# Second product of the second MLP by Strassen's algorithm in an attention, MLP, MLP kernel on one core

## Chip, core and metric

The kernel runs on one core of one Trainium2 chip. The metric is the device time of one launch in microseconds (us), the median of several runs. The engines are PE (TensorE, matrix products; its weight loads are PEld), DVE (VectorE), ACT (ScalarE), POOL (GpSimd), and SP, whose queue issues all the DMAs.

## What is computed

```python
def _attn_ref(q, k, v, tau) -> np.ndarray:
    scale = 1.0 / np.sqrt(q.shape[-1])
    scores = scale * np.matmul(q, k.transpose(0, 1, 3, 2))
    thresh = np.max(scores, axis=-1, keepdims=True) - tau
    scores = np.where(scores >= thresh, scores, -1000000000.0)
    scores = scores - np.max(scores, axis=-1, keepdims=True)
    attn = np.exp(scores)
    attn = attn / (np.sum(attn, axis=-1, keepdims=True) + 1e-09)
    return np.matmul(attn, v).astype(np.float32)
...
def _moe_ref(x, w_in, w_out, alpha) -> np.ndarray:
    h = x @ w_in
    g = np.maximum(h, 0.0) + alpha * np.minimum(h, 0.0)
    return (g @ w_out).astype(np.float32)
...
def _moe2_ref(x, w_in, w_out) -> np.ndarray:
    h = x @ w_in
    g = h - np.tanh(h)
    return (g @ w_out).astype(np.float32)
...
    x = np.ascontiguousarray(attn_out.transpose(0, 2, 1, 3)).reshape(B * S, H * D)
    x = _moe_ref(x=x, **moe_kwargs)
    return _moe2_ref(x=x, **moe2_kwargs)
```

All of it is float32: 4 batches of 8 heads with 576 rows of 64, so 2304 tokens of 512; either MLP goes from 512 to 2048 and back.

## The kernel before

The 2304 tokens are nine blocks of 256 (`BLK`, `NBLK`). A fast matrix product takes operands rounded to the type `fp32r`, so each float32 operand is split into a rounded part hi and the rest lo, and a product is three: hi·hi, hi·lo, lo·hi. The 64 visits of the attention (a batch, a query block of 256 and a head each; `attend`) and 16 visits for the last 64 queries of two heads (`attend_left`) run softmax over rows of 576: row maximum, threshold, exponential, mask with row sum, guard, reciprocal, normalisation (`softmax`), then transposes on PE and the product with v (`products`). For the first `WHOLE` visits that product is one exact float32 product without any split (`one`), for the first `RAW` the scores are (`raw`); later visits use split operands. As soon as all eight heads of a block are there, the first MLP's work on that block runs between the attention's instructions.

An MLP block is eight pairs of inner chunks (`NPAIR`; a pair is 2 x 128 of the 2048 inner columns). `h_pair` makes a pair's first product, 24 products of 256 columns into the PSUM bank `hp`; then come the activation function into `mr` (ACT and DVE), the rounded copy `gh` (line 278) and the rest `gl` (line 283). `acc_pair` makes the second product from `gh`, `gl` and the weights. In the first MLP that is 24 products of 256 columns (line 957), in the second 12 products of 512 columns into `acc[0]` and `acc[1]` (line 949). `LEAD = 2`: the second product of a pair stands two pairs behind its first. After the eighth pair ACT copies `acc` out (`drain`) and SP stores it.

The weights come as 64-bit words of float64 numbers, which lines 333 to 351 turn into float32 (`rebias`, `three`, `ends_`, `middle`); then `hi` and `lo` split them (`piece`). Those of the second MLP take the places of the first's as these come free, so they are prepared in the stretch after the attention.

The order on every engine is written out ahead of time by a planner (`Plan.order`). Each operation has engines that may do it with an assumed cost (`any_of`, `either`: ACT, DVE or POOL), a rank (a number that grows with the place in the program, shifted by the constants `OFF`, `MLP_PE`, `MLP_G`, `PREP`, `PA`, `PB`, `XR`), and what it reads, writes and takes of buffers (`BUFS`). The planner always issues the operation that can start first, of several the one with the lowest rank; `POOL_PEN`, `ACT_PEN` and `DVE_PEN` are added when it compares engines. It takes POOL and a DVE operation that reads SBUF alone as excluding each other (`port_free`). 280 products on zeros (`warm`) fill PE where nothing else can run; they are used up within the first 150 us.

Of the kernel before, what the change touches and what calls it, by code (L numbers as in the profile page):

```python
# [22 lines left out]
P = 128  # L23
# [34 lines left out]
DVE_PEN = 0.9665  # L58
OFF = {"S": 22.48, "M": -53.36, "TH": -421.88, "E": -13.37, "X": -179.21, "R": -223.53, "N": 37.71, "T": 278.13, "H": -180.15, "L": -303.91, "AV": 69.42, "XC": -10.5, "XH": 126.9}
# [3 lines left out]
    "rkv": 1, "rq": 2, "ks": 3, "qs": 2, "vs": 3, "e": 2, "st": 2, "eT5": 1, "xt": 1, "rw": 4, "raw0": 2, "raw1": 4, "tw": 2,  # L63
    "x0": 2, "x1": 2, "mr": 1, "pair": 1, "xl": 1, "gh": GB, "gl": GB, "o": 2,
# [8 lines left out]
class Plan:  # L73
# [9 lines left out]
    def add(self, engines, rank, emit, reads=(), writes=(), banks=(), takes=(), lag=0.0, after=(), port=False):  # L83
# [19 lines left out]
        for tag, _ in takes:  # L103
            if tag != "rw":
                if tag in self.takers:
                    order.add(self.takers[tag])
                self.takers[tag] = n
        deps.discard(n)
        self.ops.append((engines, rank, emit, deps, order - deps, banks, takes, lag, "DVE" in engines and not banks and engines["DVE"] > 0.1))
        return n  # L110

    def order(self):
# [41 lines left out]
        issued = []  # L154
        pen = {"ACT": ACT_PEN, "DVE": DVE_PEN, "POOL": POOL_PEN}
        while len(issued) < n:
            best = None
            for e, cand in ready.items():
# [35 lines left out]
                key = (t + (pen[e] if len(ops[i][0]) > 1 else 0), fin)  # L194
# [34 lines left out]
def attention_mlp_mlp(ctx: ExitStack, tc: tile.TileContext, kv, q0, q1, tau, w1i, w1o, alpha, w2i, w2o, out):  # L229
# [37 lines left out]


# [43 lines left out]
    def piece(l, kind, qd, c, rank):  # L312
# [3 lines left out]
        raw, t, dst = ("raw", n), ("tw", n), ("w", (l, kind, qd))  # L316
# [37 lines left out]

        def hi(e):
# [48 lines left out]
    def prep(v, rank):  # L404
# [720 lines left out]
```

## Time and profile before

| | us |
|---|---|
| median of 3 runs (lowest, highest) | 1168.94 (1168.88, 1170.43) |
| the profiled execution, its own time | 1169.88 |
| its span | 1168.1 |
| PE busy in the span | 1141.2 (98%) |
| DVE, ACT, POOL busy | 662.9, 663.6, 525.5 |

A busy PE instruction lasts until its last column has left the array, so records of neighbours overlap: what an instruction costs PE is the distance from its start to the next start. On the other engines neighbours overlap by less than 0.1 us. The stages are the attention with most of the first MLP in it (0 to about 660 us), the rest of the first MLP (to about 760) and the second MLP.

### The profile page before, as it was taken

Reading aid. Unit: us, or ns where it says so; the run is one execution under the profiler, and the core shown is the slowest. Engines: PE = TensorE matmul, PEld = TensorE weight load, DVE = VectorE, ACT = ScalarE, POOL = GpSimd, SP = SyncE. Lnnn points to the kernel's source line nnn. Section 1 sums busy time; section 2 is a strip of 40 time slices with the busy share of each in tenths; the row PEclk is TensorE's granted clock in tenths of the full one; section 3 lists DMA queues with packets and bytes.
Section 4 is the critical chain, followed back from the end, with each engine's and each line's share of the span. In section 5 each row is a group of like instructions: output and inputs, shape, how many; then the busy total and the mean of one; then the engine's idle time right before and its main releaser. Section 6 shows DMA issues by size and latency. Waiting matters only on the chain.

```text
span 1168.1 us, 21647 instructions
## 1 busy us (share of the span) xinstructions
PE 1141.2 (98%) x8388; PEld 1051.9 (90%) x8388; DVE 662.9 (57%) x1388; ACT 663.6 (57%) x1277; POOL 525.5 (45%) x498
## 2 busy tenths in 40 slices
PE   8999999999999999999999999999999999999998
PEld 6777789899999999999999999999899999999997
DVE  5887787888887877878877665782111111111110
ACT  5887887677776767767677565664222233222221
POOL 2565564544555525556535375875233233233221
PEclk9999999999999999999999999999999999999999
DMA  6645533212122302132121353451011011010000
GB/s 177 188 159 160 159 107 100 55 49 64 54 65 84 86 13 80 54 92 81 46 70 41 95 163 127 141 167 55 1 37 36 1 36 37 1 37 18 1 19 19
DMA packets 55847, 86.88 MB, mean 74 GB/s; under 512 B 18624, under 2 KB 33984, under 8 KB 55744
## 3 DMA queue, kind: packets, MB, share of 16 engines
q1 hardware_dynamic: 55744, 85.49, 24.2%
q8 instruction: 66, 1.08, 0.4%
q14 instruction: 37, 0.30, 0.1%
HBM read 75.51 MB, written 9.96 MB: 73 GB/s over the span
## 4 chain that ended last, share of the span: by engine, by line
PE 72%; DVE 15%; ACT 8%; issue 3%; DMA 2%; SPq 1%; POOL 0%; DVEq 0%; ACTq 0%; POOLq 0%
PE hp L896 29%; PE acc L949 17%; PE acc L957 11%; PE sc L720 3%; DVE e L565 3%; PE pt L615 3%; DVE eT L283 3%; PE sc L689 2%; DVE st L553 2%; DMA rw<-in_w1i_dram 2%; ACT eT L278 1%; ACT e L561 1%; DVE st L570 1%; PE sc L681 1%; DVE mr L917 1%
## 5 line engine op out<-in xcount | busy, mean ns | idle before, releaser
L896 PE MATMUL hp<-x,ihi 128*128 128x256 f32 x2304 | 426.4, 284 | 1.7 <-DVE mr L917 1.6
L896 PEld LDWEIGHTS hp<-x,ihi 128*128 128x128 f32 x2304 | 358.9, 189 | 9.3 <-issue 1.4
L283 POOL TENSOR_TENSOR gl<-mr,gh 128x512 fp32r<-128x512 f32 x144 | 193.7, 1345 | 360.0 <-ACT gh L278 340.3
L896 PE MATMUL hp<-x,ilo 128*128 128x256 f32 x1152 | 323.9, 281 | 0.0
L915 DVE TENSOR_TENSOR mr<-hp,mr 128x512 f32<-128x512 f32 x72 | 49.8, 691 | 325.0 <-ACT mr L908 325.0
L896 PEld LDWEIGHTS hp<-x,ilo 128*128 128x128 f32 x1152 | 217.5, 189 | 0.0
L908 ACT ACTIVATE mr<-hp 128x512 f32<-128x512 f32 x72 | 43.1, 598 | 223.4 <-PE hp L896 223.4
L957 PE MATMUL acc<-gh,ohi 128*128 128x256 f32 x576 | 168.2, 292 | 0.5 <-ACT o L278 0.5
L957 PE MATMUL acc<-gl,ohi 128*128 128x256 f32 x576 | 161.8, 281 | 0.0
L957 PE MATMUL acc<-gh,olo 128*128 128x256 f32 x576 | 161.6, 281 | 0.0
L565 DVE SCALAR_TENSOR_TENSOR e<-sc,st,e 128x576 f32<-128x576 f32 x144 | 115.2, 814 | 21.1 <-ACT e L561 9.6
L278 ACT ACTIVATE gh<-mr 128x512 fp32r<-128x512 f32 x133 | 83.8, 630 | 73.9 <-DVE mr L915 48.8
L553 DVE TENSOR_REDUCE st<-sc 128x1 f32<-128x576 f32 x144 | 106.0, 749 | 17.4 <-PE sc L681 6.5
L949 PE MATMUL acc<-ohi,gl 128*128 128x512 f32 x288 | 113.8, 395 | 0.0
L949 PE MATMUL acc<-olo,gh 128*128 128x512 f32 x288 | 113.7, 395 | 0.0
L949 PE MATMUL acc<-ohi,gh 128*128 128x512 f32 x288 | 113.5, 394 | 0.0
L561 ACT ACTIVATE e<-sc,st 128x576 f32<-128x576 f32 x144 | 103.8, 739 | 10.8 <-DVE st L553 8.3
L957 PEld LDWEIGHTS acc<-gh,ohi 128*128 128x128 f32 x576 | 109.0, 189 | 0.9 <-ACT o L278 0.8
L957 PEld LDWEIGHTS acc<-gl,ohi 128*128 128x128 f32 x576 | 108.7, 189 | 0.0
L957 PEld LDWEIGHTS acc<-gh,olo 128*128 128x128 f32 x576 | 108.5, 188 | 0.0
L615 PE MATMUL pt<-ident,e 128*128 128x128 f32 x576 | 88.6, 276 | 6.4 <-ACT e L278 2.2
L278 ACT ACTIVATE e<-e,st 128x576 f32<-128x576 f32 x95 | 71.9, 771 | 40.3 <-DVE st L573 40.0
(91 smaller groups left out, 1948.5 us busy)
## 6 DMA issues: line engine op xcount, KB each, us to landing
rkv<-in_kv_dram SPq DMA_DIRECT2D x36, 288.0 KB, 2.8
rw<-in_w1i_dram SPq DMA_DIRECT2D x16, 512.0 KB, 4.8
rw<-in_w1o_dram SPq DMA_DIRECT2D x16, 512.0 KB, 4.0
rw<-in_w2i_dram SPq DMA_DIRECT2D x16, 512.0 KB, 4.5
rw<-in_w2o_dram SPq DMA_DIRECT2D x16, 512.0 KB, 3.5
rkv<-in_kv_dram SPq DMA_DIRECT2D x44, 160.0 KB, 2.9
ks<-in_kv_dram SPq DMA_DIRECT2D x20, 288.0 KB, 3.0
x1d<-o SPq DMA_DIRECT2D x18, 256.0 KB, 2.1
```

The lines of the kernel that those rows point to most:

```text
L278: e.activation(out=out_, in_=in_, func=AF.Copy, **({} if scale is None else {"scale": scale}))
L283: e.tensor_tensor(out=out_, in0=in_, in1=hi.bitcast(F32), op=ALU.subtract)
L553: e.tensor_reduce(out=T[st][:, 0, j:j + 1], in_=x(s), axis=AX.X, op=ALU.max, negate=True)
L561: e.activation(out=weights(j), in_=x(s), func=AF.Exp, bias=T[st][:, 0, j:j + 1], scale=1.0)
L565: e.scalar_tensor_tensor(out=w_, in0=x(s), scalar=T[st][:, 1, j:j + 1], in1=w_, op0=ALU.is_ge, op1=ALU.mult, accum_out=T[st][:, 2, j:j + 1])
L615: e.transpose(pt[:, c, :], x[:, c * P:(c + 1) * P], ident)
L720: e.matmul(po, lhsT=vf[:, c], rhs=T[g][part][:, c, :], start=(c + part == 0), stop=False)
L896: e.matmul(hp[:, k, :], lhsT=weight(l, "i", part, f // 4)[:, c, (f % 4) * P:(f % 4 + 1) * P], rhs=T[f"x{x}", m][:, c, :], start=(n0 + n == ...
L908: e.activation(out=T[r], in_=hp, func=AF.Tanh)
L915: e.tensor_tensor(out=T[r], in0=hp, in1=T[r], op=ALU.subtract)
L949: e.matmul(acc[t], lhsT=g[:, k, t * P:(t + 1) * P], rhs=w, start=(f == 0 and n == 0), stop=(f == NF - 1 and n == 2),)
L957: e.matmul(acc[t][:, (c % 2) * BLK:(c % 2 + 1) * BLK], lhsT=w[:, c * P:(c + 1) * P], rhs=g[:, k, :], start=(f == 0 and n == 0 and c % 2 == ...
```

## The change

In the second MLP a pair is a 2 x 2 problem: two halves of 128 tokens, two chunks of the inner dimension, two halves of 256 output columns. For six of the eight pairs (`STRASSEN`) its second product is made in seven products instead of eight, in Winograd's form of Strassen's algorithm: four sums of quarters of `mr` (`combine`, tile `gs`, 128 x 128 each), four sums of quarters of the weight (made once, `out_pair`), the split of all seven operands on either side, and 7 x 3 products of 256 columns into the four banks of the former score tiles `sc`. Pairs 1 and 7 keep 12 products of 512 columns, into the same banks. After a block, ACT copies one sum, and DVE adds the rest up in six operations before the store.

`h_pair` of the second MLP alternates between the banks `hp` and `pt` (the transposes' bank, free by then). The second product there stands one pair behind the first (`LEAD = (2, 1)`). A Strassen pair takes two of the three `g` buffers. All ranks and penalties of the planner are new, `WHOLE` grows from 14 to 19 and `RAW` falls from 22 to 20; some assumed costs are raised, and operations marked `late` (splits of the second MLP, its weights, all `g`) are compared with other penalties (0.8 us for POOL, none for DVE).

```diff
+STRASSEN = (0, 2, 3, 4, 5, 6)
...
-TA = 16.6305
-PA, PB = 26.706, 2.665
-MLP_PE = 1031.4114
...
-WHOLE = 14
-RAW = 22
+TA = 15.1927
+PA, PB = 272.298, 4.647
+MLP_PE = 1230.3142
...
+WHOLE = 19
+RAW = 20
...
-POOL_PEN = 0.1305
-ACT_PEN = 0
+POOL_PEN = 0.3611
+ACT_PEN = 0.1795
...
-LEAD = 2
+LEAD = (2, 1)
...
-DVE_PEN = 0.9665
+DVE_PEN = 0.2288
...
+        late_pen = {"ACT": 0.1, "DVE": 0.0, "POOL": 0.8}
...
-                key = (t + (pen[e] if len(ops[i][0]) > 1 else 0), fin)
+                key = (t + ((late_pen if ops[i][9] else pen)[e] if len(ops[i][0]) > 1 else 0), fin)
...
+    hps = hp, pt.rearrange("p (k c) s -> p k (c s)", k=2)
...
+        hq = hps[l * (p % 2)]
...
-        add({"DVE": 0.13}, rank + OFF["TH"], threshold, [*[(*st, 0, j) for j in js], ("const", 0), ROOM], [(*st, 1)])
+        add({"DVE": 0.21}, rank + OFF["TH"], threshold, [*[(*st, 0, j) for j in js], ("const", 0), ROOM], [(*st, 1)])
...
-        add({"DVE": 0.08}, rank + OFF["R"], guard, [*[(*st, 2, j) for j in js], ROOM], [(*st, 3)])
+        add({"DVE": 0.11}, rank + OFF["R"], guard, [*[(*st, 2, j) for j in js], ROOM], [(*st, 3)])
...
+        def combine(e, n):
+            if not n:
+                take(epool(), sums, [P, 2, BLK], F32, "gs", BUFS["gs"])
+            x, y = ((0, 2), (4, 1), (1, 0), (3, 5))[n]
+            e.tensor_tensor(out=quarter(4 + n), in0=quarter(x), in1=quarter(y), op=ALU.subtract if n else ALU.add)
...
+    def out_products(p, rank):
...
+        seven = [(0, 0, 1), (2, 1, 2), (1, 6, 4), (3, 3, 5), (4, 4, 6), (5, 5, 7), (6, 2, 3)]
...
+        def emit_seven(e, now):
+            gh, gl = T[g], T["gl", p]
+            wh, wl = T[w]
+            for a, b, number in now:
+                a, b = slice(a * P, (a + 1) * P), slice(b * BLK, (b + 1) * BLK)
+                out_, bank = half_bank(number)
+                for i, (x, y) in enumerate(((gl, wh), (gh, wh), (gh, wl))):
+                    e.matmul(out_, lhsT=x[:, a], rhs=y[:, b], start=(n == 0 and i == 0 and number in (1, 2, 5, 4)),
+                             stop=(n == NPAIR - 1 and i == 2), skip_group_check=True)
...
+        add({"ACT": 0.3}, r, p1, [("c", 0)], oa + [o[0], o[1]], [("c", 0)], takes=[("o", x) for x in o])
+        add({"DVE": 0.35}, r, lambda e: total(e, b(), bank(6), a()), [("c", 0), *oa], ob, [("c", 0)])
...
+            add({"DVE": 0.6}, r, both, [("c", x), *z], z, [("c", x)])
...
-                    if l:
-                        for n, (g, w) in enumerate(((gh, hi), (gh, lo), (gl, hi))):
-                            e.matmul(
-                                acc[t], lhsT=g[:, k, t * P:(t + 1) * P], rhs=w,
-                                start=(f == 0 and n == 0), stop=(f == NF - 1 and n == 2),
-                            )
-                        return
```

What stands where, at the three places that matter. First PE at the last pairs of the second MLP before; `x`, `ihi`, `ilo` are the first product's operands, `acc_91` and `acc_92` the two output banks.

```order
L896 MATMUL hp<-x_12398,ilo_9973 128x256
L949 MATMUL acc_91<-ohi_9809,gh 128x512
L949 MATMUL acc_91<-olo_9810,gh 128x512
L949 MATMUL acc_91<-ohi_9809,gl 128x512
L949 MATMUL acc_92<-ohi_9809,gh 128x512
L949 MATMUL acc_92<-olo_9810,gh 128x512
L949 MATMUL acc_92<-ohi_9809,gl 128x512
```

PE at the same place now, after the first product of pair 7 (`pt`), at the second product of pair 6 (`wp` are the weight's seven parts, `g` those of the activations; `sc_89`, `sc_90` hold two banks each).

```order
L975 MATMUL pt<-x_13044,ilo_9673 128x256
L1084 MATMUL sc_89<-wp_9841,g 128x256 x2
L1084 MATMUL sc_89<-wp_9842,g 128x256
L1084 MATMUL sc_89<-wp_9841,g 128x256 x2
L1084 MATMUL sc_89<-wp_9842,g 128x256
L1084 MATMUL sc_90<-wp_9841,g 128x256 x2
L1084 MATMUL sc_90<-wp_9842,g 128x256
L1084 MATMUL sc_90<-wp_9841,g 128x256 x2
L1084 MATMUL sc_90<-wp_9842,g 128x256
```

Twelve products of 512 columns have become 21 of 256, and behind the last first product PE has two second products left, where before it had three. Next DVE in the second MLP before, from the last weights on:

```order
L351 SCALAR_TENSOR_TENSOR tw<-tw,rw 128x512
L346 SCALAR_TENSOR_TENSOR rw<-rw 128x512
L915 TENSOR_TENSOR mr<-hp,mr 128x512
L351 SCALAR_TENSOR_TENSOR tw<-tw,rw 128x512
L915 TENSOR_TENSOR mr<-hp,mr 128x512 x65
```

DVE there now, one pair and the start of the next:

```order
L994 TENSOR_TENSOR mr<-hp,mr 128x512
L1033 TENSOR_TENSOR gs<-mr 128x128
L1033 TENSOR_TENSOR gs<-gs,mr 128x128
L1033 TENSOR_TENSOR gs<-mr 128x128
L1033 TENSOR_TENSOR gs<-mr,gs 128x128
L290 TENSOR_TENSOR g<-mr,g 128x384
L290 TENSOR_TENSOR g<-gs,g 128x512
L994 TENSOR_TENSOR mr<-pt,mr 128x512
```

One instruction a pair has become seven: the four sums, and the two `lo` passes, which POOL did before. Last DVE in the attention before, in the middle of it:

```order
L570 TENSOR_SCALAR st<-st 128x2
L573 RECIPROCAL st<-st 128x2
L553 TENSOR_REDUCE st<-sc_89 128x1
L734 TENSOR_TENSOR xt<-sc_90,xt 64x256
L553 TENSOR_REDUCE st<-sc_90 128x1
L556 TENSOR_SCALAR st<-st,atau 128x2
L474 SCALAR_TENSOR_TENSOR qs<-rq,qscale,qs 128x256
L283 TENSOR_TENSOR eT_5082<-pt,eT_5081 128x4x128
```

DVE in the middle of the attention now:

```order
L646 TENSOR_SCALAR st<-st 128x2
L290 TENSOR_TENSOR ks<-rkv,ks 64x640
L649 RECIPROCAL st<-st 128x2
L287 TENSOR_SCALAR vs<-rkv 128x5x64
L656 TENSOR_SCALAR e<-e,st 128x576
L290 TENSOR_TENSOR eT_4884<-pt,eT_4883 128x4x128
L290 TENSOR_TENSOR eT_4888<-sc_89,eT_4888 64x128 x2
L810 TENSOR_TENSOR xt<-sc_89,xt 64x256
```

Splits of keys and values (`ks`, `vs`) and normalisations (`e<-e,st`), which POOL and ACT did, now stand between the softmax's own steps on DVE. Counted over the program, POOL has 503 instructions before and 220 now, DVE 1246 and 1951.

## Rows read from the trace of the kernel before

**Rows 1.** The page, part 1: busy us, share of the span, instructions.

```profile
PE 1141.2 (98%) x8388; PEld 1051.9 (90%) x8388; DVE 662.9 (57%) x1388; ACT 663.6 (57%) x1277; POOL 525.5 (45%) x498
```

**Rows 2.** Stretches: length, busy PE, PEld, DVE, ACT, POOL (instructions), clock, DMA share, GB/s.

```profile
660.00:760.00 100.00, 100.00 (x847) 100.00 (x846) 60.90 (x79) 59.83 (x103) 66.53 (x49) 1.00 0.45 145
760.00:1160.00 400.00, 400.00 (x2553) 361.59 (x2552) 72.40 (x91) 120.43 (x196) 129.71 (x91) 1.00 0.10 32
0.00:660.00 660.00, 638.42 (x4982) 588.43 (x4982) 529.61 (x1218) 482.15 (x977) 329.23 (x358) 1.00 0.31 89
```

**Rows 3.** The chain that ended last, from 1140 us: start, length, work.

```profile
1145.93 2.84 PE hp L896 x24
1148.77 2.80 PE acc L949 x12
...
1154.41 8.41 PE acc L949 x36
...
1162.85 0.60 ACT o L278
```

**Rows 4.** PE in order of time in the attention: start, length, instruction.

```profile
67.20 2.51 PE L712 MATMUL acc<-eT,vs 128*64 128x256 f32 x10
69.65 1.24 PE L681 MATMUL sc<-ks,qs 64*128 64x320 f32 x8
...
151.94 1.94 PE L810 MATMUL sc<-eT,vs 128*64 128x64 f32 x20
153.81 0.38 PE L957 MATMUL acc<-gh,ohi 128*128 128x256 f32 x1
...
302.99 1.19 PE L720 MATMUL sc<-eT,vs 128*128 128x256 f32 x8
...
304.13 0.28 PE L957 MATMUL acc<-gh,ohi 128*128 128x256 f32 x1
...
316.29 1.23 PE L810 MATMUL sc<-eT,vs 128*128 128x128 f32 x10
317.36 0.74 PE L689 MATMUL sc<-ks,qs 128*128 128x320 f32 x4
```

**Rows 5.** All engines in order of time, one pair of the second MLP.

```profile
900.25 0.28 PE L896 MATMUL hp<-x,ilo 128*128 128x256 f32 x1
...
900.63 0.60 ACT L908 ACTIVATE mr<-hp 128x512 f32<-128x512 f32 x1 [2.30 <-PE hp L896]
...
901.26 0.69 DVE L915 TENSOR_TENSOR mr<-hp,mr 128x512 f32<-128x512 f32 x1 [4.95 <-ACT mr L908]
...
901.98 0.63 ACT L278 ACTIVATE gh<-mr 128x512 fp32r<-128x512 f32 x1 [0.76 <-DVE mr L915]
...
902.69 1.29 POOL L283 TENSOR_TENSOR gl<-mr,gh 128x512 fp32r<-128x512 f32 x1 [4.35 <-ACT gh L278]
```

**Rows 6.** DVE, then POOL, in order of time around 303 us.

```profile
302.75 1.00 DVE L474 SCALAR_TENSOR_TENSOR qc<-rq,qscale,qc 128x64 fp32r<-128x64 f32 x1
...
302.10 1.57 POOL L283 TENSOR_TENSOR ks<-rkv,ks 64x640 fp32r<-64x640 f32 x1
```

**Rows 7.** Groups by line and shape: count, busy us, mean ns, idle before.

```profile
L474 DVE SCALAR_TENSOR_TENSOR qc<-rq,qscale,qc 128x64 fp32r<-128x64 f32 x24 | 7.4, 315 | 1.2 <-ACT qc L278 1.2
...
L570 DVE TENSOR_SCALAR st<-st 128x2 f32<-128x2 f32 x64 | 27.8, 434 | 1.1
...
L570 DVE TENSOR_SCALAR st<-st 128x1 f32<-128x1 f32 x16 | 2.4, 148 | 0.2
...
L580 POOL TENSOR_SCALAR e<-e,st 128x576 f32<-128x576 f32 x49 | 38.7, 790 | 69.6 <-DVE st L573 63.6 <-PE sc L810 4.4 <-PE sc L689 0.6
...
L283 POOL TENSOR_TENSOR x<-rw,x 128x1024 fp32r<-128x1024 f32 x10 | 24.4, 2444 | 0.3 <-ACT x L278 0.3
```

**Rows 8.** Two stretches of the attention, columns as in rows 2.

```profile
150.00:180.00 30.00, 29.98 (x244) 27.51 (x245) 25.74 (x58) 24.59 (x52) 15.83 (x16) 1.00 0.38 113
...
390.00:420.00 30.00, 28.42 (x228) 27.09 (x226) 26.64 (x63) 19.82 (x41) 16.35 (x17) 1.00 0.16 45
```

More of the change, by code (lines that the diff above doesn't have):

```diff
@@ L108, in add @@
         deps.discard(n)
-        self.ops.append((engines, rank, emit, deps, order - deps, banks, takes, lag, "DVE" in engines and not banks and engines["DVE"] > 0.1))
+        self.ops.append((engines, rank, emit, deps, order - deps, banks, takes, lag, "DVE" in engines and not banks and engines["DVE"] > 0.1, late))
         return n
@@ L353, in middle, with piece @@
             )
+        add({"SYNC": P * 4096 / DMA_RATE}, rank, load, reads=[("products", NV - 1), ("products", -NV)] * l, writes=[raw, (*raw, 0)], takes=[("rw", raw), (f"raw{l}", raw)], lag=DMA_LAG)
+        add(any_of(0.575, 0.335, 0.59), rank, rebias, reads=[raw], writes=[t], takes=[("tw", t)], late=l)
+        add(any_of(0.56, 0.59, 0.62), rank, three, reads=[raw], writes=[(*raw, 0)], late=l)
+        add({"DVE": 0.64}, rank, ends_, reads=[raw, (*raw, 0)], writes=[(*raw, 0)])
+        add({"DVE": 0.64}, rank, middle, reads=[(*raw, 0)], writes=[t])
+        return t
+    def piece(l, kind, qd, c, rank):
+        t, dst = turned_float(l, kind, qd, c, rank), ("w", (l, kind, qd))
         def hi(e):
@@ L935, in h_pair, with hi, lo @@
-        add(any_of(0.52, 0.335, 0.59), rank, hi, [(*r, 0), (*r, 1)], [gh], takes=[("gh", gh)])
-        add(either(0.6, 1.23) if FLEX or not l else {"DVE": 0.6}, rank, lo, [(*r, 0), (*r, 1), gh], [gl], takes=[("gl", gl)])
+                add({"DVE": 0.4}, rank, lambda e, k=k: second(e, k), [hpk, ("const", 3)], [(*r, k)], hb)
+        both = [(*r, 0), (*r, 1)]
+        if not l or p % NPAIR not in STRASSEN:
+            def hi(e):
+                copy(e, take(apool, g, [P, 2, 2, BLK], F32R, "g", BUFS["g"])[:, 0], T[r])
+            def lo(e):
+                sub(e, T[g][:, 1], T[r], T[g][:, 0])
+            add(any_of(0.52, 0.335, 0.59), rank, hi, both, [(*g, 0)], takes=[("g", g)], late=l)
+            add(either(0.62, 1.3), rank, lo, [*both, (*g, 0)], [(*g, 1)], late=l)
+            return
@@ new lines, in lo @@
+        def lo(e, n):
+            if not n:
+                take(apool, gl, [P, 7 * P], F32R, "g", BUFS["g"])
+            x = (T[sums] if n else T[r]).rearrange("p a s -> p (a s)")
+            a = slice(3 * P, 7 * P) if n else slice(0, 3 * P)
+            sub(e, T[gl][:, a], x if n else x[:, P:], T[g][:, a])
+        for n in range(4):
+            add({"DVE": 0.21}, rank, lambda e, n=n: combine(e, n), both + [(*sums, 0)] * (n in (1, 2)) + [(*sums, 1)] * (n == 3),
+                [(*sums, n)], takes=[] if n else [("gs", sums)])
@@ new lines, in h_pair @@
+        for n in range(2):
+            z = [(*sums, x) for x in range(4)] if n else both
+            h1 = add(any_of((0.42, 0.52)[n], (0.27, 0.335)[n], (0.46, 0.59)[n]), rank, lambda e, n=n: hi(e, n), z, [(*g, n)],
+                     takes=[] if n else [("g", g)], after=[h1] if n else [], late=True)
+            l1 = add(either((0.46, 0.6)[n], (0.93, 1.23)[n]), rank, lambda e, n=n: lo(e, n), [*z, (*g, n)], [(*gl, n)],
+                     takes=[] if n else [("g", gl)], after=[l1] if n else [], late=True)
```

255 lines of the change are left out of this document (182 added, 73 removed).

## Prediction

> **What bounds the kernel now.** I read four views. The page's first part shows PE busy in 98% of the span and every other engine below 60% [rows 1], so the kernel is a queue of matrix products, and the question is where PE is not streaming. The table of stretches answers it [rows 2]: from 660 us to the end of the second MLP PE is busy for every microsecond, at a granted clock of 1.00 (the 2.4 GHz level), while DVE works 72 us of 400, ACT 120 and POOL 130. Before 660 us PE shows 21.6 us of idle time and DVE is the fullest of the others, 530 us of 660. The chain of waits for the end is PE alone, one pair after the other: 24 first products in 2.84 us, 12 second products in 2.80 us [rows 3]. So a product of 256 columns costs PE 0.118 us and one of 512 costs 0.233 us, and in the second MLP every product taken away is time taken away, provided that operands come in time. The time line gives that condition [rows 5], and the rows around 303 us show what can hold DVE up [rows 6].
>
> **The change part by part.**
>
> *Strassen's products.* A pair costs 21 x 0.118 = 2.49 us in place of 2.80, so 0.315 us less; 9 blocks x 6 pairs make 54 of them: **-17.0 us**, all of it on the path. A rule speaks against this step: the Trainium skill (TensorE: Matmul & The Clock Gate, section Back-to-back issue gap) gives, for a stream of load and product pairs, 131 ns a product at 512 columns and 81 at 128. By it half the columns cost more than half (about 98 ns at 256, an estimate interpolated from that page), 21 would take 2.06 us against 1.57, and the sum would get +26 us instead of -17. The trace has 233 and 118 ns in this very stage, so the measurement decides; as a rival it stands below with next to no chance.
>
> *Exact attention.* `WHOLE` from 14 to 19: five visits change their product with v from nine split instructions, 1.14 us (302.99 to 304.13), to five exact ones, which are ten in the trace and take 2.45 us (67.20 to 69.65) [rows 4]: 5 x 1.31 = +6.6 us. Two halves of the visits for the last 64 queries change too: 1.07 us for the split form of two heads (316.29 to 317.36), 1.87 us for twenty instructions of the exact form (151.94 to 153.81), so two heads cost 2 x 0.4 = +0.8 us. `RAW` 22 to 20 swaps two visits' scores from one form to another of nearly the same length (eight exact instructions take 1.24 us with their tail); I count it at nothing. PE gets **+7.4 us**. DVE loses 5 visits' splits of the transposed weights, about 13 us.
>
> *The wait at the end.* PE now stands one pair behind. From the last first product to `gl` ready the time line has 0.38 us, tanh 0.60, `mr` 0.69, `gh` 0.63 and `gl` 1.29, in all 3.73 us [rows 5]; the last pair is a plain one with `gl` on DVE (the same 512 columns as `mr`, 0.69), so 3.1 us, and only pair 6 stands before it, 2.49 + 0.12 us. **+0.5 us** (bounds 0 and 1.1, with the POOL row's 1.29). The final DVE addition takes the place of ACT's 0.60 us copy [rows 3], 0.69: nothing.
>
> *The chain in the other pairs.* A Strassen pair needs 0.38 + 0.60 + 0.69, then four sums of 128 x 128 (no such row; the nearest is DVE's 128 x 64 group, 0.315 with its waits [rows 7], and I take 0.22 each, since it holds locked instances), rounding 0.63 and `lo` 0.69: about 4.0 us, 4.4 at 0.315. PE is then busy with the previous second product and the next first one, 2.49 + 2.84 = 5.3 us. So it is hidden with 0.9 to 1.3 us to spare, and the second bank for first products takes `hp` off the list of what is waited for. What can eat the margin is POOL: DVE's 64 columns took 1.00 us at 302.75, until POOL's pass ended at 303.67 [rows 6], so a DVE instruction on SBUF alone waits for a whole POOL pass. POOL's only work in the second MLP is now the `lo` of a new x, 2.44 us [rows 7], seven times. If each delays the sums by its full length PE waits 7 x (2.4 - 1.2) = 8 us; if it falls beside the `mr` of another pair, nothing. **+1.5 us** (0 to 8), nearer to nothing: the planner takes a POOL pass and such a DVE pass as excluding each other, so its order can place products of another pair there.
>
> *Weights for the second MLP.* From the last attention instruction to pair 5's weights DVE's order holds some 240 instructions: 123 passes of 512 columns at 0.69 us (85), 61 of 256 or 384 at about 0.45 (28), 20 of 128 columns (5), 29 scalar passes at 0.42 (12; this price is explained with the attention), two of 1024 columns (2.5): 132 us. PE's order up to the first use has 1068 products of 256 columns and 12 of 512, 129 us. In the stretch before, DVE had 39 us to spare out of 100 [rows 2]; that is gone. Neighbours overlap a little (-7 us), POOL's five passes there lock DVE (up to +8 us), so PE waits between 0 and 9 us; I take **+3 us**. This term replaces a stretch without any wait.
>
> *The attention's gaps.* DVE takes over from POOL and ACT: 40 normalisations, 18 `lo` of keys, 28 `gl`, 20 of v, 18 of x, 47 passes for weights and 13 `gh`, 18 small sums, some 90 us with passes of two sources at DVE's 0.69 us per 512 columns [rows 5] and scalar passes at 0.42, the middle between the one-column scalar pass, 0.148 [rows 7], and that 0.69 (no row is nearer). DVE goes from 530 to about 605 us of 660. POOL falls from 329 us to about 185. For a gain: the guard of the row sum, two columns, takes 434 ns on the mean and 148 in the one-column form that seldom meets POOL [rows 7], 64 x 0.29 = 18 us of waiting on the way from scores to transposes; fewer POOL passes lift part of it, and the planner's costs for these steps come nearer to the rows. Normalising on DVE also saves the wait for it (POOL stood 63.6 us waiting for the reciprocal). For a loss: a DVE 92% full. The stretches bound it: at 150 us, DVE 25.7 of 30, PE is idle for 0.02 us; at 390 us, DVE 26.6, for 1.58 us [rows 8]. All 22 stretches like the first would be -21 us, like the second +13 us. I take **-6 us**: PE's idle stretches do not follow DVE's load in those rows, and the guard's wait is a real part of it.
>
> The sum: -17.0 + 7.4 + 0.5 + 1.5 + 3 - 6 = -10.6 us. The profiled execution took 1169.88 us (span 1168.1), 0.94 above the median, so it gives 1159.3 in such an execution and **1158 us** as the median.
>
> **The rivals.**
>
> *A: DVE bounds the attention (slower).* The scalar passes that go to DVE have no DVE row; POOL's normalisation took 0.79 us [rows 7], and at that price some 100 passes cost 0.35 us more each than counted. DVE then needs 640 us of 660, 97%, and the gaps grow past the worst stretch, +13 to +25 in place of -6: 1158 + 25 = 1183 us. It decides from about 0.95 of DVE's time on. Against it: in the rows a DVE at 0.89 did not slow PE as a rule. The Trainium skill (VectorE: DVE Perf Modes, section Mode 2x_2P) says that a float32 pass with one SBUF source and a scalar runs at two elements a cycle, which speaks against this rival; the trace of before has no such pass on DVE.
>
> *B: the gain is given back by waits (about the same).* Weights late by 9 us, x passes 8 us and no gain in the attention: 1158 + 6 + 6.5 + 6 = 1176 at the very worst, half of that 1167. For it: the 132 against 129 us. Against it: PE's order there draws three first products ahead of the late weights.
>
> *C: the attention's gaps close.* With PE as idle as at 150 us: 1158 - 15 = 1143 us.
>
> *D: half-width products cost more than half*, as the Trainium skill's figures would have it: 1158 + 43 = 1201 us.
>
> **How the numbers follow.** Forecast (1150 to 1166) 0.57, C and in between 0.18, B 0.12, A 0.12, D 0.01. Changes under 0.2% (2.3 us) can't be told from none here. Faster: forecast, C and a part of B, 0.78; the same: most of B around 1167 to 1171, 0.08; slower: A, D and the rest of B, 0.14. The range reaches to C's time and to B's middle: 1143 to 1168.
>
> **What would show it.** Line 1084's groups at 0.118 us a product and no PE idle from 780 us on: the first term. PE's idle time between 660 and 790 us: the weights. PE idle in bursts once a block beside POOL's x: the lock. DVE's share before 660 us, its 128 x 576 scalar pass at 0.4 or 0.7 us, and the two-column guard back near 150 ns: the attention. The prediction is wrong if DVE is busy over 95% before 660 us, or if second products wait for `g` in most pairs.

## The result, and the profile after

The changed kernel takes **1153.6 us** (median of four runs, 1152.4 to 1156.3) beside 1169.7 us for the kernel before on the same chip: ratio 0.9861, 95% interval [0.9849, 0.9873], 16 us less. Faster, as forecast, and 4 us below the forecast 1158, inside the range. The profiled execution is the slowest of the four (1156.25 us, span 1154.5), so its span shows 13.6 us of the gain and not 16.

First the page's first part of the kernel after, then its stretches (columns as in rows 2), to be read against [rows 1] and [rows 2]:

```profile
PE 1126.2 (98%) x8889; PEld 1065.3 (92%) x8889; DVE 919.6 (80%) x2093; ACT 640.6 (55%) x1237; POOL 214.4 (19%) x215
```

```profile
660.00:760.00 100.00, 99.62 (x842) 99.42 (x841) 86.86 (x167) 58.01 (x100) 10.10 (x5) 1.00 0.49 155
760.00:1160.00 400.00, 384.30 (x3028) 372.59 (x3027) 244.42 (x531) 127.30 (x218) 14.95 (x6) 0.99 0.10 33
0.00:660.00 660.00, 642.24 (x5024) 593.30 (x5025) 588.27 (x1395) 455.32 (x920) 189.39 (x204) 1.00 0.30 89
...
760.00:790.00 30.00, 26.77 (x210) 25.67 (x210) 28.91 (x66) 19.04 (x35) 0.00 (x0) 1.00 0.45 141
790.00:820.00 30.00, 28.66 (x206) 26.11 (x205) 22.97 (x51) 10.35 (x18) 0.00 (x0) 1.00 0.16 53
820.00:1140.00 320.00, 320.00 (x2556) 313.00 (x2555) 186.06 (x402) 96.27 (x164) 14.95 (x6) 1.00 0.06 21
```

PE is still the queue that sets the time. DVE went from 57% to 80% of the span, POOL from 45% to 19%. Where PE had no idle time at all before [rows 2], it now has 4.6 us between 760 and 820 us, 3.2 of them in the 30 us where DVE is 96% busy; from 820 to 1140 us it has none.

The chain of waits at the end (start, length, work), in the place of [rows 3]:

```profile
1122.25 2.45 PE sc L1084 x21
1124.70 2.84 PE hp L975 x24
1127.54 2.45 PE sc L1084 x21
1129.98 2.84 PE pt L975 x24
...
1143.40 2.46 PE sc L1084 x21
...
1146.78 3.05 PE sc L1091 x12
```

A Strassen pair (line 1084, 21 products) takes 2.45 us in the place of 2.80 for 12 wide ones, pair after pair.

To split the time I take two marks from PE's rows: the start of the last second product of the first MLP, and the start of the first second product of the second MLP's second block. They divide each span into the attention with the first MLP, the second MLP's first block, and its other eight with the end. The columns add up to the span; the last two are the median of the runs and the profiled execution's mean granted clock. The three columns are one execution each. One of the ten runs of e_w14_pens took 1231 us at a mean clock of 0.844, where the others had 0.986 to 0.992; without it that median is 1165.4.

| kernel | attention, first MLP | block 1 | blocks 2 to 9, end | span | median | clock |
|---|---|---|---|---|---|---|
| before | 762.1 | 45.2 | 360.8 | 1168.1 | 1169.7 | 0.999 |
| after | 759.5 | 50.1 | 344.9 | 1154.5 | 1153.6 | 0.998 |
| c_after (the same again) | 756.6 | 50.3 | 344.9 | 1151.8 | 1154.5 | 0.998 |
| e_plain | 759.0 | 45.2 | 359.6 | 1163.8 | 1164.6 | 0.998 |
| e_late_relief | 759.0 | 46.5 | 343.8 | 1149.3 | 1149.6 | 0.999 |
| e_relief_prep | 756.6 | 48.3 | 343.1 | 1148.0 | 1149.8 | 0.998 |
| e_lock_twice | 758.4 | 52.4 | 349.0 | 1159.8 | 1161.4 | 0.996 |
| e_short_exact | 752.4 | 51.3 | 344.9 | 1148.6 | 1152.3 | 0.996 |
| e_whole14 | 762.8 | 50.5 | 345.0 | 1158.3 | 1161.8 | 0.998 |
| e_pens | 754.6 | 57.5 | 343.2 | 1155.3 | 1160.0 | 0.997 |
| e_w14_pens | 764.5 | 56.3 | 343.3 | 1164.1 | 1165.6 | 0.989 |
| e_b_whole19 | 767.6 | 45.2 | 360.7 | 1173.5 | 1175.0 | 1.000 |
| e_oldranks | 765.8 | 54.7 | 343.9 | 1164.4 | 1166.5 | 0.989 |
| e_oldranks_w19 | 768.8 | 54.4 | 343.8 | 1167.0 | 1167.2 | 0.992 |

Before to after: -2.6, +4.9 and -15.9 us. The last is mainly the products: 48 pairs x 0.35 = 16.8 us less. Of the 0.9 us that are missing to it, most is late weights again, in block 2: with these waits relieved (e_late_relief) the column is 343.8, 17.0 less than before. The middle one holds 6 x 0.35 = 2.1 us less work, so by the marks 7.0 us of waiting are new there (4.6 us show as PE's idle time). Five kernels have the same order on all engines up to 660 us (after, c_after, e_plain, e_late_relief, e_lock_twice); their first column is 756.6 to 759.5, mean 758.5. Part of that spread is the clock: in the first 30 us it was 0.94 in after and 1.00 in c_after, which is up to 1.8 us.

### The profile page after: what moved, and what is told of

Its sections match the earlier page's. It is cut to its first block, busy times and chain, and to the rows that moved or that the text cites. A ratio compares the mean times of both kernels' runs of the same rounds, so it can differ in the third digit from the quotient of the medians.

```text
span 1154.5 us, 23027 instructions
## 1 busy us (share of the span) xinstructions
PE 1126.2 (98%) x8889; PEld 1065.3 (92%) x8889; DVE 919.6 (80%) x2093; ACT 640.6 (55%) x1237; POOL 214.4 (19%) x215
## 3 DMA queue, kind: packets, MB, share of 16 engines
q1 hardware_dynamic: 55712, 85.62, 24.5%
## 4 chain that ended last, share of the span: by engine, by line
PE 79%; DVE 12%; ACT 4%; DMA 2%; issue 2%; POOL 1%; SPq 0%; ACTq 0%; DVEq 0%; POOLq 0%
PE hp L975 21%; PE acc L1162 14%; PE sc L1084 10%; PE pt L975 8%; PE pt L691 4%; PE sc L1091 4%; PE sc L765 3%; PE sc L796 3%; PE acc L1211 2%; PE sc L788 2%; DVE eT L290 2%; DVE e L641 2%; PE sc L757 2%; PE sc L886 2%; DVE st L629 1%
## 5 line engine op out<-in xcount | busy, mean ns | idle before, releaser
L975 PE MATMUL hp<-x,ihi 128*128 128x256 f32 x1728 | 323.0, 285 | 0.5 <-DVE mr L996 0.5
L975 PEld LDWEIGHTS hp<-x,ihi 128*128 128x128 f32 x1728 | 265.3, 189 | 1.4 <-DVE mr L996 0.7
L1162 PE MATMUL acc<-g,ohi 128*128 128x256 f32 x1152 | 217.2, 286 | 0.4 <-ACT o L285 0.4
L1162 PEld LDWEIGHTS acc<-g,ohi 128*128 128x128 f32 x1152 | 176.6, 189 | 1.4 <-issue 0.7
L1162 PE MATMUL acc<-g,olo 128*128 128x256 f32 x576 | 161.9, 281 | 0.0
L1084 PE MATMUL sc<-wp,g 128*128 128x256 f32 x1134 | 143.3, 280 | 3.9 <-DVE g L290 1.8
L1084 PEld LDWEIGHTS sc<-wp,g 128*128 128x128 f32 x1134 | 137.2, 188 | 5.3 <-DVE g L290 2.2
L1162 PEld LDWEIGHTS acc<-g,olo 128*128 128x128 f32 x576 | 108.5, 188 | 0.0
L975 PE MATMUL pt<-x,ihi 128*128 128x256 f32 x576 | 104.1, 281 | 0.0
L975 PEld LDWEIGHTS pt<-x,ihi 128*128 128x128 f32 x576 | 89.7, 189 | 1.4
L285 ACT ACTIVATE g<-mr 128x384 fp32r<-128x384 f32 (+1 forms) x98 | 56.3, 574 | 52.5 <-DVE mr L994 36.4
```

What stands on the lines that cost most here:

```text
L285: e.activation(out=out_, in_=in_, func=AF.Copy, **({} if scale is None else {"scale": scale}))
L975: e.matmul(hq[:, k, :], lhsT=weight(l, "i", part, f // 4)[:, c, (f % 4) * P:(f % 4 + 1) * P], rhs=T[f"x{x}", m][:, c, :], start=(n0 + n == ...
L1084: e.matmul(out_, lhsT=x[:, a], rhs=y[:, b], start=(n == 0 and i == 0 and number in (1, 2, 5, 4)), stop=(n == NPAIR - 1 and i == 2), skip_g ...
L1162: e.matmul(acc[t][:, (c % 2) * BLK:(c % 2 + 1) * BLK], lhsT=w[:, c * P:(c + 1) * P], rhs=g[:, k, :], start=(f == 0 and n == 0 and c % 2 == ...
```

## The experiments

**c_after.** The changed kernel again, on the chip of e_plain, e_pens and e_whole14. The other edits ran on two other chips; on the three the kernel before took 1169.4 to 1170.1 us.

> The changed kernel itself once more, on the chip of the next three, so that they have something to be compared with: 1153.6 us (1152.4 to 1156.3 in its first runs), PE idle some 5 us between 780 and 810 us where the second MLP's first weights are used.

Measured: 1154.5 us, ratio 0.9875 [0.9862, 0.9887]. It serves as the reference.

**e_plain: no Strassen pairs.**

```diff
-STRASSEN = (0, 2, 3, 4, 5, 6)
+STRASSEN = ()
...
-                e.matmul(two_banks(3 - 2 * t), lhsT=x, rhs=y, start=False, stop=(n == NPAIR - 1 and k == 1 and i == 2), skip_group_check=True)
+                e.matmul(two_banks(3 - 2 * t), lhsT=x, rhs=y, start=(n == k == i == 0), stop=(n == NPAIR - 1 and k == 1 and i == 2), skip_group_check=True)
...
-                total(e, T[o[t]], two_banks(x), T[o[t]])
+                copy(e, take(apool, o[t], [P, 512], F32, "o", BUFS["o"]), two_banks(x))
```

> All eight pairs plain, every other number as in the changed kernel: no sums of quarters of g or of the weights, 12 products of 512 columns a pair, the results drained by one copy a bank. Theory 1 (the products are the gain): 54 pairs x (2.80 - 2.45) = 18.9 us more on TensorE, and the wait for the first weights of the second MLP, about 5 us, goes with the sums and the longer roundings: 1153.6 + 18.9 - 5 = 1167 us (1164 to 1173). Rival (the new ranks and the second bank are what made the kernel faster, the products are hidden behind waits): within 4 us of the changed kernel, 1150 to 1158 us.

Measured: 1164.6 us, 10 us above c_after. The chain that ended last of e_plain shows the old price again, and 24 wide products in 5.61 us at the end:

```profile
1150.73 2.84 PE pt L975 x24
1153.57 5.61 PE sc L1091 x24
```

So theory 1 stands: two thirds of the gain are the products, net of the waits that they bring. By the table blocks 2 to 9 lose 14.7 us and block 1 gains 5.1, because the waits go (PE idles 0.8 us in the 400 from 760 us on, all the rest is work). The attention's part is untouched.

```profile
760.00:1160.00 400.00, 399.17 (x2541) 360.58 (x2540) 154.34 (x250) 63.76 (x103) 0.00 (x0) 1.00 0.08 27
```

**e_late_relief and e_relief_prep: passes of the second MLP off DVE.**

```diff
-        late_pen = {"ACT": 0.1, "DVE": 0.0, "POOL": 0.8}
+        late_pen = {"ACT": 0.0, "DVE": 0.3, "POOL": 0.5}
```

> The changed kernel with other penalties for the second MLP's passes alone (ACT 0.0 in place of 0.1, DVE 0.3 in place of 0.0, POOL 0.5 in place of 0.8): some 35 scalar passes go from DVE to ACT and a few passes to POOL, so that DVE, busy 29 of 30 us from 750 to 780 us, has room. Theory (PE's 6.7 us of waiting between 780 and 810 us is DVE's work on the weights being late): the wait falls to 2 to 4 us, 1150 to 1152 us. Rival (the chain of one weight or of g is too long whatever DVE's load, or POOL's lock takes back what is freed): the wait stays at 6 to 8 us, 1153 to 1156 us.

Measured: **1149.6 us**, ratio 0.983 [0.9815, 0.9845], clear of the changed kernel's interval. PE's rows in order of time, first of after, then of e_late_relief (in brackets the idle time before a row and what ended it):

```profile
782.56 0.65 PE L1084 MATMUL sc<-wp,g 128*128 128x256 f32 x3 [0.32 <-DVE wp L290]
784.37 1.79 PE L1084 MATMUL sc<-wp,g 128*128 128x256 f32 x13 [1.16 <-DVE wp L290]
787.92 2.75 PE L1084 MATMUL sc<-wp,g 128*128 128x256 f32 x21 [1.76 <-DVE g L290]
```

```profile
780.99 2.62 PE L1084 MATMUL sc<-wp,g 128*128 128x256 f32 x21
784.25 2.74 PE L1084 MATMUL sc<-wp,g 128*128 128x256 f32 x21 [0.64 <-DVE g L290]
789.66 2.64 PE L1084 MATMUL sc<-wp,g 128*128 128x256 f32 x21
```

The stretches of e_late_relief:

```profile
760.00:790.00 30.00, 29.36 (x237) 28.68 (x236) 29.40 (x66) 22.03 (x41) 4.60 (x3) 1.00 0.34 112
790.00:820.00 30.00, 29.14 (x219) 27.39 (x218) 20.35 (x45) 10.74 (x18) 1.30 (x1) 1.00 0.16 54
```

PE's idle time between 760 and 820 us falls from 4.6 to 1.5 us, block 1 from 50.1 to 46.5. So most of the waits were DVE's lateness with the weights and with g behind them; ACT had room for the scalar passes. This order, 20 us under the kernel before, and the next one are the fastest found.

e_relief_prep goes further:

```diff
-PREP = -52.0122
+PREP = -86.77
...
-        late_pen = {"ACT": 0.1, "DVE": 0.0, "POOL": 0.8}
+        late_pen = {"ACT": 0.0, "DVE": 0.41, "POOL": 0.46}
```

> e_late_relief a step further: penalties of the second MLP's passes ACT 0.0, DVE 0.41, POOL 0.46 (there 0.0, 0.3, 0.5), and the splits of q, k and v ranked 35 earlier (PREP -86.8 in place of -52.0). Theory (the weights' passes on DVE are still the last wait, and earlier splits leave DVE room at the end of the attention): PE's waits from 780 to 820 us at or below the 2.6 us of e_late_relief, the last attention product no later, 1146 to 1149 us. Rival (what is left of the waits is the chain of one pair and the drains, whoever does the passes): 1149 to 1151 us, the same as e_late_relief.

Measured: 1149.8 us, ratio 0.982 [0.9801, 0.9839]: the rival's number, no further gain. Its reason isn't shown: the edit changes two things, and by the table the first column is 2.4 us shorter than in e_late_relief and block 1 is 1.8 longer.

**e_lock_twice: POOL's pass on x doubled.**

```diff
             sub(e, T["x1", m], x(), T["x0", m])
+            if m > NBLK and e is nc.gpsimd:
+                sub(e, T["x1", m], x(), T["x0", m])
```

> The changed kernel, but in the second MLP POOL makes the lower part of each new x twice over, so that its seven passes of 2.44 us that can hold DVE up become 4.9 us each. Theory (the sums of g have 1 us and more to spare, and the order keeps POOL's pass off them): no change, 1152 to 1156 us. Rival (the lock is on the path, as the prediction's 0 to 8 us allowed): each block 1.2 to 2.4 us later, 1162 to 1171 us.

Measured: 1161.4 us, ratio 0.9928 [0.9913, 0.9944], 7 us more; between the two, nearer the rival. In after one sum of each block already stands behind POOL, for nothing. After, POOL and then DVE in order of time:

```profile
850.46 2.45 POOL L290 TENSOR_TENSOR x<-rw,x 128x1024 fp32r<-128x1024 f32 x1 [90.47 <-DVE gs L1033]
```

```profile
850.37 0.29 DVE L1033 TENSOR_TENSOR gs<-mr 128x128 f32<-128x128 f32 x1
850.57 2.49 DVE L1033 TENSOR_TENSOR gs<-mr,gs 128x128 f32<-128x128 f32 x1
852.98 0.68 DVE L1117 TENSOR_TENSOR o<-sc,o 128x512 f32<-128x512 f32 x1
853.76 0.69 DVE L290 TENSOR_TENSOR g<-gs,g 128x512 fp32r<-128x512 f32 x1
```

The same place in e_lock_twice, POOL, DVE and PE:

```profile
851.71 4.92 POOL L290 TENSOR_TENSOR x<-rw,x 128x1024 fp32r<-128x1024 f32 x2 [92.79 <-ACT x L285]
```

```profile
851.81 2.49 DVE L1035 TENSOR_TENSOR gs<-mr,gs 128x128 f32<-128x128 f32 x1
854.23 0.68 DVE L1119 TENSOR_TENSOR o<-sc,o 128x512 f32<-128x512 f32 x1
855.01 2.17 DVE L290 TENSOR_TENSOR g<-gs,g 128x512 fp32r<-128x512 f32 x1
```

```profile
857.24 1.69 PE L1086 MATMUL sc<-wp,g 128*128 128x256 f32 x12 [0.41 <-DVE g L290]
```

A sum of 128 columns takes 2.49 us in place of 0.29 while POOL works, and behind the second pass the rounding's lower part takes 2.17 in place of 0.69, which is 1.5 us more. Blocks 2 to 9 lose 4.1 us, six times about 0.7. So some 0.8 us of a block's margin were still free, and the single pass costs nothing there. The seventh pass, doubled too, lies just ahead of block 1, at 754 us, where DVE is full. There two of DVE's passes take 2.77 and 2.88 us in place of 0.69, and block 1 loses another 2 us. In after it was POOL that stood behind DVE at this place (5.04 us for the pass of 2.45).

**e_pens: POOL's work back in the attention.**

```diff
-POOL_PEN = 0.3611
-ACT_PEN = 0.1795
+POOL_PEN = 0.1305
+ACT_PEN = 0
...
-DVE_PEN = 0.2288
+DVE_PEN = 0.9665
```

> The planner's penalties for work on POOL, ACT and DVE in the attention and the first MLP set back to those of the kernel before (0.1305, 0, 0.9665); ranks, products and everything else as in the changed kernel. 180 instructions go back to POOL and some 45 to ACT. Theory 1 (PE's gaps in the attention came from DVE standing behind POOL's passes): the guard of two columns, now 228 ns, goes back to about 430 ns, PE gets most of the 10 us of gaps back before 660 us: 1160 to 1164 us. Rival (the ranks closed the gaps, who does the passes is of no account): 1152 to 1156 us.

Measured: 1160.0 us, the number of theory 1, but not for its reason. One group of e_pens, to be read against [rows 7], and its stretch:

```profile
L646 DVE TENSOR_SCALAR st<-st 128x2 f32<-128x2 f32 x64 | 23.4, 366 | 0.8
```

```profile
0.00:660.00 660.00, 645.96 (x5067) 597.24 (x5067) 510.40 (x1194) 474.41 (x960) 341.25 (x374) 1.00 0.30 89
```

The guard is back at 366 ns (after has 228), DVE down to 77%, and the attention with the first MLP is not slower: 754.6 us, the shortest of all kernels that do the full work. What this execution lost it lost in block 1 (57.5), at the weights, where the clock fell too:

```profile
780.00:810.00 30.00, 24.62 (x156) 21.59 (x157) 25.38 (x54) 11.70 (x20) 2.37 (x1) 0.89 0.12 43
```

The profiled execution is the fastest of the four (1157.2 us, mean clock 0.997; the others 0.991 to 0.994), so where the others lost their 2 to 4 us more isn't seen. In this one the guard's wait, on which I had put part of the attention's gain, is not on PE's path: PE idles 14.0 us of the first 660, after 17.8.

**e_whole14, e_w14_pens, e_b_whole19, e_short_exact: the exact visits.**

```diff
-WHOLE = 19
-RAW = 20
+WHOLE = 14
+RAW = 22
```

That is e_whole14; e_w14_pens has the penalties of e_pens besides.

> The exact visits as in the kernel before (14 whole visits and 22 raw ones in place of 19 and 20), all else as in the changed kernel. Theory 1 (the exact products are 7.4 us of pure work on TensorE, and DVE has room for the 13 us of splits that come back): 1153.6 - 7.4 = 1146 us (1144 to 1149). Rival (with DVE 89% full before 660 us the splits come late and PE waits as long as it saves): 1152 to 1158 us.

Measured: 1161.8 us, ratio 0.9945 [0.9926, 0.9965], 7 us slower with 7.4 us less work on PE, and not the 7 us faster of my theory. I then blamed DVE's load, 596 us of 660:

> Both edits of the last two runs together: 14 whole and 22 raw visits, and the penalties of the kernel before, so that POOL takes some 200 passes off DVE. e_whole14 lost 7 us although it has 7.4 us less work on TensorE. Theory 2 (it lost them because DVE, 90% full, made the splits of the five visits late): with DVE at about 78% the loss goes, the last attention product starts at 655 us or earlier, the kernel is at or below e_pens: 1153 to 1159 us. Rival (a split visit has the longer chain from scores to products, and PE runs out of other work meanwhile, whoever does the passes): the last attention product starts at 662 us or later, 1163 to 1168 us.

Measured: 1165.6 us, ratio 0.9969 [0.9958, 0.998], with DVE at 521 us of 660 and PE idle for 22.7 of them (e_whole14 22.4). Theory 2 fell as well, and its rival's numbers came: 1163 to 1168 us, the last attention product at 666.6. That rival, the longer chain of a split visit, was put to the kernel before as a rule for any order (`WHOLE` 19 and `RAW` 20 there, nothing else):

> The kernel before with 19 whole and 20 raw visits, nothing else changed. Theory (exact products are pure work on PE's path, as the prediction counted them): 1169.4 + 7.4 = 1176.8 us (1174 to 1179). Rival (their shorter chain saves as much as they cost, whatever the order): 1162 to 1171 us.

Measured: 1175.0 us, ratio 1.005 [1.0034, 1.0066]: 5.6 us slower. There the exact visits are work on the path, as the prediction priced them, so the rival falls as a rule for any order; for the new one it stays possible. Last, the changed kernel's order with part of that work taken out:

```diff
-                for c in range(5):
+                for c in ((0, 4) if 14 <= 16 * bb + 8 * qq + (7 - hh if qq else hh) else range(5)):
```

> The changed kernel's order, instruction for instruction, but in the five visits that became exact the product with v is made for two of the five chunks of keys alone (the other three are left out of the sum). Each exact product takes 0.49 us, so TensorE has 5 x 3 x 0.49 = 7.3 us less work in the attention and no other engine has less. Theory (exact products are pure work on PE's path, 7.4 us as the prediction counted): 7 us less than the changed kernel, 1147 us (1145 to 1149). Rival (PE waits at these places for softmax steps anyway, and the products fill the wait): within 2.5 us of the changed kernel, 1151 to 1156 us.

Measured: 1152.3 us, ratio 0.9855 [0.9839, 0.9872]. By the numbers laid down this is the rival's: of 7.3 us the median gives back 2 against c_after, with intervals that overlap. But the first column is 4 us shorter than c_after's and 6 shorter than the mean of the five, and block 1 is then 1 us longer. c_after is the nearer measure, since both kept the full clock up to the mark: there some 4 of the 7.3 us are on PE's path. Over all the runs it is between 2 and 6.

**e_oldranks and e_oldranks_w19: the old numbers.** All of the planner's numbers that both kernels have (`TA`, `PA, PB`, `MLP_PE`, `MLP_G`, `PREP`, `XR`, `OFF`, `LAG` and the three penalties) as before; the second with `WHOLE` 19 and `RAW` 20.

> The changed kernel with all of the planner's numbers of the kernel before that have a counterpart (ranks, offsets, penalties, lags, whole and raw visits); Strassen's products, the second bank and the changed costs stay. Theory 1 (second MLP minus 10 us by itself, as e_plain showed, the attention as in the kernel before): the last attention product starts near 660 us and the kernel takes 1157 to 1161 us. Rival (the second MLP's gain needs the new ranks, since the old ones bring its weights or its g too late): PE waits over 10 us more after 760 us, 1165 us or more.

Measured: 1166.5 us, ratio 0.9973 [0.9959, 0.9988]. Theory 1's 1157 to 1161 is wrong, and so is the rival's reason: block 1 is no more than 5 us longer, the attention with the first MLP is 6 to 9 us longer than with the new ranks.

> e_oldranks, but with the changed kernel's 19 whole and 20 raw visits. In the changed kernel with its own ranks the last attention product starts at 656 to 659 us, with 14 whole visits at 665 us, with the old ranks and 14 whole visits at 667 us. Theory (the exact visits spare the attention its waits under any ranks): 658 to 662 us here, 1157 to 1162 us in all. Rival (ranks and visits belong together, and the old ranks with other visits are worse still, as the kernel before lost 5.6 us with 19): 667 to 675 us, 1166 to 1174 us.

Measured: 1167.2 us, ratio 0.9973 [0.9959, 0.9987], the rival. So the exact visits cost under the old ranks (+3.0 and +5.5 us in the first column, 765.8 to 768.8 and 762.1 to 767.6) and pay under the new ones (762.8 to 758.5; in the medians 1161.8 to 1154.5). Ranks and visits are good only together.

Where e_oldranks loses its time can be seen. Its stretches from 175 us on (the granted clock is the third number from the end), and PE's rows there:

```profile
175.00:180.00 5.00, 3.06 (x22) 1.97 (x21) 2.65 (x6) 2.38 (x7) 1.57 (x2) 0.99 0.60 200
180.00:185.00 5.00, 3.96 (x16) 2.87 (x14) 2.79 (x8) 2.16 (x5) 0.00 (x0) 0.50 0.08 17
185.00:190.00 5.00, 3.79 (x16) 3.29 (x18) 2.29 (x7) 2.31 (x4) 2.72 (x4) 0.50 0.01 3
190.00:195.00 5.00, 5.00 (x30) 4.35 (x29) 2.75 (x7) 2.66 (x8) 0.31 (x1) 0.64 0.41 111
```

```profile
175.42 1.24 PE L757 MATMUL sc<-ks,qs 64*128 64x320 f32 x8
...
179.59 0.86 PE L691 MATMUL pt<-ident,e 128*128 128x128 f32 x4 [1.91 <-DVE eT L290]
181.14 2.59 PE L796 MATMUL sc<-eT,vs 128*128 128x256 f32 x8 [0.69 <-ACT eT L285]
186.21 2.39 PE L886 MATMUL sc<-eT,vs 128*128 128x128 f32 x10 [1.41 <-DVE eT L290]
188.53 2.29 PE L757 MATMUL sc<-ks,qs 64*128 64x320 f32 x8
```

PE waits 1.91 us for a split, then 0.69, and the granted clock is 0.50, the 1.2 GHz level, for some 13 us: the same eight score products take 1.24 us at 175 and 2.29 us at 189. In these rows 2.5 + 2.5 + 1.8 = 6.8 us of the full clock are missing, so up to that much of the 6 to 9 us is clock.

## Why the prediction was right, step by step

**Strassen's products** (-17.0): right mechanism, a little small. 54 x (2.80 - 2.45) = -18.9 us, since 256 columns take 0.1167 us in this stream and not 0.118. Half the columns cost half the time, so rival D is out.

**Weights for the second MLP** (+3, bounds 0 to 9): right mechanism and nearly the place (the first waits stand at pairs 3 and 4, counted from 0, and not at 5), sized too small. 7.0 us of new waiting in block 1, where DVE is 28.91 us of 30 busy; e_late_relief gives back 3.6 us of it in block 1 and 1.1 in block 2, 4 to 5 us in the medians. The count was good: in after the 238 DVE records between 661.3 us and the use of pair 5's weights at 793.3 add up to 136 us (132 forecast). Neighbours overlap by 17 us and not by 7. What the term put at nothing is DVE standing idle, 13.5 us of these 132: between 660 and 760 us it is busy 86.86 of 100, and 7.6 us of the idle time end with ACT's part of the first MLP's activation. Rival B was right in this half.

**The lock by POOL** (+1.5, 0 to 8): nothing from block 2 on, the lower bound. The hold-up is there once a block, and covered with some 0.8 us to spare (e_lock_twice). It falls into a sum and not beside the `mr` of another pair, so the order didn't avoid it; the margin took it. That margin, 0.9 to 1.3 us by the prediction, was of the right size for a pair without a hold-up: in after one such pair has the last part of g ready at 867.85, and PE starts on it at 869.17. The sum is held 2.2 us, more than that, and still costs nothing: nine of the pair's 21 products run before the last rounding is wanted (in e_lock_twice PE's wait stands before the other 12). The Trainium skill (SBUF — State Buffer, section Who interferes with whom) says that a DVE instruction with two SBUF inputs contends with a GpSimd instruction that reads SBUF, for ports that one of them holds alone. The trace agrees: the sum began 0.11 us later than POOL's pass of 2.45 us and ended 0.15 us later.

**The wait at the end** (+0.5, 0 to 1.1): PE waits 0.93 us, by another cause than the one named. After, DVE, ACT and PE in order of time:

```profile
1145.25 0.69 DVE L290 TENSOR_TENSOR g<-mr,g 128x512 fp32r<-128x512 f32 x1
1145.88 0.38 ACT L285 ACTIVATE o<-sc 128x256 f32<-128x256 f32 x1 [1.85 <-PE sc L1084]
1146.30 1.67 DVE L1117 TENSOR_TENSOR o<-sc,o 128x256 f32<-128x256 f32 x4 [0.36 <-ACT o L285]
1146.78 3.04 PE L1091 MATMUL sc<-wp,g 128*128 128x512 f32 x12 [0.93 <-DVE o L1117]
```

The last g is ready at 1145.94, 0.1 us after PE stopped, where 0.5 was costed. PE starts only after ACT's copy and DVE's first sum of the half banks, which the order puts ahead of the last plain products; they lie in the same `sc` tile. Whether that order can be turned round without a longer drain wasn't tried. The drain, which the prediction left as it was, is 0.6 us shorter: from PE's last product to the end of the span 5.27 us before, 4.65 after. So the end as a whole costs about 0.3 us.

**Exact attention** (+7.4) and **the attention's gaps** (-6), together +1.4: measured -2.6, and -3.6 on the mean of five. The two can be told apart by adding up PE's rows up to the mark, each from its start to the next start. The products with v take 7.7 us more than before in after and 6.8 in c_after, so the price of the exact visits was right. All the rest takes 10.3 and 12.3 us less, with nearly the same instructions, where 6 was forecast: 5.1 of it behind the transposes, 4.7 and 5.5 behind the first MLP's second products. Of that gain of 10 us and more only 3.8 show as PE's idle time before 660 us (21.6 before, 17.8 after); the rest are waits too short for it. So the gaps' term was sized too small, and its reason does not hold, though the sum of both terms is within the bounds. The exact visits cost what was priced in the order of before (e_b_whole19, +5.6 for 7.4). In the new one a part of their time is filled up again by waits (e_short_exact), and a kernel planned without them is 7 us slower (e_whole14): its order has more waits than the products are long. The reason for the gaps' gain, fewer waits of DVE behind POOL, is not borne out: the guard did fall from 434 to 228 ns, but it goes back to 366 in e_pens and PE loses nothing before the second MLP in its profiled execution. Nor does DVE's load decide: at 77% (e_pens) and 89% the first column is the same within 5 us. Rival A, a DVE that bounds the attention, is out: DVE was 89% full (588.27 of 660), its 128x576 scalar pass took 0.63 us on the mean, near the dear end, and PE idled less. Rival C, gaps as small as at 150 us (-21), came halfway at most. What the new ranks do to shorten these waits stays open; that it is they (with `OFF` and `LAG`), and only with the exact visits, is what e_oldranks, e_oldranks_w19 and e_whole14 show, since the penalties by themselves (e_pens) leave the first column as short.

**The sum.** Second MLP: -12.0 forecast, 4.9 - 15.9 = -11.0 measured, the larger gain of the products and the larger wait for the weights nearly cancelling, which is luck. The rest: +1.4 forecast, -2.6 in the profiled execution; with the other four it is -3.6, and the medians, which differ by 16, give it 1 us more. So the forecast of 1158 missed by the attention's part: the gaps closed by 10 to 12 us and not by 6.

## What to carry to other kernels

On this stream of products without gaps the count of columns was the price, and Strassen's seven for eight is worth its 12% of that stream; but its sums and the longer roundings fall on the one vector engine, and the first block, where the weights are still being made, pays for them. After such a change look for the first stretch in which the vector engine is full and move scalar passes off it there, which was worth another 4 us here. A planner's ranks, penalties and the choice of work they were found with can't be judged one at a time: each group of them put back made this kernel slower (the ranks were put back only together with the penalties).

## What was not expected of the hardware

**A wait of PE can cost twice.** In e_oldranks two waits close together were followed by half the clock (rows above), and it isn't one execution's chance. All ten runs of e_oldranks had a mean granted clock of 0.987 to 0.992, the four of after 0.997 or 0.998, the kernel before 0.997 to 1.000. At 0.989 of 1164 us that is 12.8 us of PE's time, against 2.3 at 0.998 of 1154 (worked out as the span times what is missing to 1); e_oldranks is 12.6 us longer than c_after. Of the 12.8 us 6.8 lie in the attention, in the rows above, and 5.1 at the first weights (0.59, 0.50 and 0.89 in the three stretches of 5 us from 790 us on), where DVE is busy 14.3 of 15 us. So over half of its loss may be clock rather than waits; e_w14_pens (0.986 to 0.992) and e_pens (0.991 to 0.997 over its runs) lose clock too. The amount of idle time alone doesn't tell it: before 660 us PE idles 24.5 us in e_oldranks and 22.4 in e_whole14, whose clock was 1.00 there.

But lost clock costs nothing where another engine sets the pace. c_after met the same wait as after at the first weights, and there the clock fell. Stretches of c_after, then PE's rows:

```profile
780.00:785.00 5.00, 3.65 (x16) 3.15 (x16) 5.00 (x10) 2.71 (x5) 0.00 (x0) 0.66 0.05 22
785.00:790.00 5.00, 4.78 (x40) 4.79 (x41) 5.00 (x15) 3.62 (x6) 0.00 (x0) 1.00 0.00 0
```

```profile
781.67 3.14 PE L1084 MATMUL sc<-wp,g 128*128 128x256 f32 x13 [1.16 <-DVE wp L290]
785.22 2.72 PE L1084 MATMUL sc<-wp,g 128*128 128x256 f32 x21 [0.41 <-DVE g L290]
```

Thirteen products took 3.14 us in place of 1.79, and the next group started 3.55 us after them in both kernels (785.22 - 781.67, 787.92 - 784.37): DVE set the pace, and the slow products used up most of the wait that after shows as 1.76 us (0.41 is left).

**DVE's scalar passes cost half as much for each column.** Groups of c_after between 660 and 800 us (mean ns behind the comma):

```profile
L290 DVE TENSOR_TENSOR g<-gs,g 128x512 fp32r<-128x512 f32 x6 | 4.1, 684 | 0.0
L1033 DVE TENSOR_TENSOR gs<-gs,mr 128x128 f32<-128x128 f32 x6 | 1.7, 285 | 0.0
L287 DVE TENSOR_SCALAR g<-gs 128x512 fp32r<-128x512 f32 x5 | 2.1, 423 | 0.0
L287 DVE TENSOR_SCALAR g<-mr 128x384 fp32r<-128x384 f32 x2 | 0.7, 354 | 0.0
```

With two sources 384 columns more cost 399 ns, 1.04 a column; with one source and a scalar 128 more cost 69, 0.54 a column. The prediction's 0.42 us for 512 columns, a middle between two far rows, was the duration itself, by luck. The Trainium skill (VectorE: DVE Perf Modes, section Mode 2×_2P) says that such a pass handles two elements a cycle; the ratio of the two slopes agrees with it.
